# Result stores queued behind a step's gate weights, the last pair's products summed in PSUM, and a conversion's roundings in another order, in an fp32 attention and two-MoE kernel

## Chip, cores and metric

One core of one Trainium2 chip. The metric is the device time of one execution in microseconds. Before the change: a median of 1690.1 us over 3 runs, 1688.39 to 1690.28.

## What is computed

```python
scale = 1.0 / np.sqrt(64)
p_packed = sm_attn(p, k, v)              # p: (8, 8, 32, 64); k, v: (8, 8, 576, 64)
out = sm_attn(q, p_packed, p_packed)     # q: (8, 8, 576, 64)
x = out.transpose(0, 2, 1, 3).reshape(4608, 512)
...
h = x @ w_in                             # 512 x 2048
g = np.maximum(h, 0) + alpha * np.minimum(h, 0)
x = g @ w_out                            # 2048 x 512
...
g = x @ w_gate                           # 512 x 1536
silu = g * (1 / (1 + np.exp(-g)))
val = x @ w_val                          # 512 x 1536
return silu * val @ w_out                # 1536 x 512
```

`sm_attn` is a softmax attention with the scale above. Everything is float32.

## The kernel before

Every float32 product is made of three matmuls (`mm3`, lines 325 to 327): each operand is split into a rounded part `hi` and a remainder `lo`, and hi·hi, hi·lo and lo·hi are added in PSUM. ACT makes `hi` by a rounding copy, POOL makes `lo` by a subtraction.

**First part (up to about 790 us).** The attention, and the first MoE in 256 `h_unit`s and `o_unit`s. An `h_unit` multiplies on PE, ACT makes `m = alpha·h` (L1084), DVE makes `g = max(...)` (L1087), ACT rounds (L1095) and POOL subtracts (L1097); an `o_unit` multiplies `g` by `w_out` into four `acc` banks. The result goes to DRAM (`x1d`).

Between these units the weights of the second MoE are converted, in pieces that fill slots of the units (`all_weights2`, a generator whose `yield "s"`, `"p"` and `"a"` are pieces of one kind each). For each of 12 steps f, `piece2` takes a raw block through ACT, DVE and POOL (`widen`: ACT Abs L243, POOL L286) into a tile `g` or `v`; `less` (L1001, POOL) makes differences of blocks in place; `split2` (ACT L983, POOL L984, then a DMA) rounds one of the seven combinations and sends it to DRAM as `wgvd` (gate and value weights) or `wo2d` (output weights). For odd f, blocks of `w_out` follow.

**Second part (about 790 to 1659 us).** The second MoE runs in 6 blocks (NBLK) of 768 tokens with 12 steps (NF2) each, 72 calls of `gv_step`. A step makes a 2 x 2 block product by seven products instead of eight; `s1` and `s2` are its two results, silu · value for two token halves. Two steps are a pair m (36 pairs). Of each pair seven forms (OUT_FORMS: A11, S3, A12, S1, S2, A22, S4, sums and differences of its `s1`, `s2`) are multiplied by the output weights, in 14 units of 3 matmuls (e = 0, 1 for each form). Units of pair m stand in the steps 2m+1 and later, at places that UNITS and FIRST_UNIT set; `between(i)` in a step calls them. A step has 42 matmuls of its own products and 21 of units, 63 in all.

The first two forms are summed over a block's pairs in PSUM (`acc0` to `acc3`). The other five go to running totals, ten slots of two SBUF tiles `sums0`, `sums1` (`total`): DVE adds each product from PSUM (`more`, L1431). With a block's last pair the totals are combined with one another (A12, S2, A22, S4, S1), transposed by DVE (`put`, L1397) and sent out by SP, four stores of 48 KB for each of 8 transposes (L1401): 32 stores a block. For a block they fall in the first steps of the next one.

**Queues.** All these DMAs are issued by SP in program order, as the scheduler of the tile framework sets it. At the end of a step n `load_gv(n + 2)` (L1229) brings the gate weights of step n + 2 in two halves, into 4 buffers that hold two steps' weights. `load_wo2` (L1238) brings output weights of pair m + 2 behind units 7 and 13. `tc.issue_after(ins)` in the code keeps an instruction from being put ahead of `ins` by the scheduler.

Of the kernel before, what the change touches and what calls it, by code (L numbers as in the profile page):

```python
# [110 lines left out]
def tile_kernel(  # L111
# [37 lines left out]
    NQ = H // HQ  # L149
    NHALF = 2 * B  # L150
    NG = NF1 // WP

    ps = ctx.enter_context(tc.tile_pool(name="ps", bufs=1, space=PSUM))
    dram = ctx.enter_context(tc.tile_pool(name="dram", bufs=1, space=DRAM))
# [1061 lines left out]
    def table():  # L1216

        nc.scalar.activation(out=spare, in_=ident[:, :1], func=AF.Silu)

    def load_gv(n):  # L1220
        if n >= NBLK * NF2:
            return
        f = n % NF2
        gvw[n] = [
            wpool.tile([P, 7, 2 * P], F32R, tag="C", name=f"gv{n}_{t}", bufs=WBUFS["C"])
            for t in range(2)
        ]
        for t in range(2):
            nc.sync.dma_start(out=f32(gvw[n][t]), in_=wgvd[f][:, t])  # L1229

    def load_wo2(m, i):

        if m >= NBLK * NF2 // 2:
# [36 lines left out]
    def gv_step(n, between):  # L1270
# [45 lines left out]
        between(5)  # L1316
        next_x("S4")
        load_gv(n + 2)

        if s + 1 < NBLK:  # L1320
            with ExitStack() as held:
# [3 lines left out]
                    if f == d:  # L1325
                        prepare_x(s + 1, name)

    both, forms, outs = {}, {}, {}
# [31 lines left out]

    def forms_last(m):

        last = m == NBLK * NF2 // 2 - 1
        a12, a22 = both[2 * m + 1]
        s2 = both[2 * m][0]
        form(m, "A22", a22)
# [19 lines left out]
                    sums[n, k] = tiles[j][:, c * T : (c + 1) * T]  # L1386
        return sums[name, e]

    def put(s, name, e):

        t, dh = dict(A12=(0, 0), S4=(0, 1), A22=(1, 0), S1=(1, 1))[name]
        if not outs:
            outs["tile"] = vp.tile([P, 4, T], F32, tag="v", name="os")
            outs["n"] = 0
        o = outs["tile"][:, outs["n"] % 4]
        outs["n"] += 1
        nc.vector.transpose(out=o, in_=total(name, e))  # L1397
        r0 = (2 * s + t) * T
        for a in range(4):
            c = 256 * dh + P * e + 32 * a  # L1400
            nc.sync.dma_start(  # L1401
                out=out[r0 : r0 + T, c : c + 32].rearrange("(b j) i -> j b i", j=32),
                in_=o[32 * a : 32 * a + 32].rearrange("p (b i) -> p b i", i=32),
            )

    def out_unit(m, i):
# [5 lines left out]
        ends = m == NBLK * NF2 // 2 - 1  # L1412
        hi, lo = forms[m, name]
        w = wo2[m, k // 4][:, k % 4]
        c = slice(e * P, (e + 1) * P)
        keeps = k < 2
        bank = bank_of(f"acc{2 * k + e}" if keeps else ("h", "at")[e])
        with behind():
            ins = mm3(
                bank,  # L1420
                (w[:, 0, c], w[:, 1, c]),
                (hi, lo),
                first or not keeps,
                last or not keeps,
                skip_group_check=True,
            )
        done(ins)
        if e and k in (3, 6):
            load_wo2(m + 2, k // 4)
        def more(to, x, engine=nc.vector):  # L1430
            engine.tensor_tensor(out=total(to, e), in0=x, in1=total(to, e), op=ALU.add)  # L1431

        if keeps:
            for to in (("A12", "S2"), ("A22",))[k] if last else ():
                more(to, bank)
            return
        if first:
            nc.scalar.activation(out=total(name, e), in_=bank, func=AF.Copy)
        else:
            more(name, bank)  # L1440
# [12 lines left out]
        put(s, name, e)  # L1453

    due_at, after_at = {}, {}
    for m in range(NBLK * NF2 // 2):
        for i in range(2 * len(OUT_FORMS)):
            d = i + FIRST_UNIT
            if m == NBLK * NF2 // 2 - 1 and i == 3:
# [3 lines left out]
        after_at[2 * m + 2, 0] = lambda m=m: forms_later(m)  # L1463
        after_at[2 * m + 2, 1] = lambda m=m: forms_last(m)

    def out_next(n, i):

        for unit in due_at.pop((n, i), ()):
            out_unit(*unit)
        if (n, i) in after_at:  # L1470
            after_at.pop((n, i))()

# [34 lines left out]
    for n, i in sorted({*due_at, *after_at}):  # L1507
        out_next(n, i)


# [35 lines left out]
```

## Time and profile before

| | |
|---|---|
| median of 3 runs | 1690.1 us |
| profiled execution | 1688.99 us |
| its span, first to last instruction | 1686.8 us |
| mean granted clock of TensorE | 0.973 |
| DVE, POOL, ACT busy | 63%, 61%, 44% |
| DMA | 195 GB/s over the span |

The profiled execution is 2.2 us longer than its span. Of TensorE's clock 1.00 is full speed, 2.4 GHz, and 0.50 is 1.2 GHz. A row of a timeline gives the start, the duration, the engine, the line and the operation with its tiles (numbers left out); in brackets stands the engine's idle time before it and what ended that. Durations of neighbours overlap: matmuls of one row take .17 us from start to start. SPq is the queue of SP, whose durations are those of issuing.

### The profile page before, as it was taken

What the parts mean: (1) busy time and instruction counts of PE and PEld (TensorE: products, weight loads), DVE (VectorE), ACT (ScalarE), POOL (GpSimd) and SP (SyncE); (2) the same over time, 40 slices, a digit from 0 to 9 for tenths busy, and PEclk for the clock granted to TensorE, in tenths of its full rate; (3) what the DMA queues carried; (4) which work ended last, traced back from release to release, by engine and by line L of the source; (5) the groups of instructions that cost most, each with busy time, mean ns of one, the idle gap of its engine ahead of it and who ended that gap; (6) DMA issues with size and microseconds to landing.
All of it is one profiled execution on the core that took longest, in us unless ns stands there. A gap on an engine that the chain in (4) does not pass through costs nothing.

```text
span 1686.8 us, 30328 instructions
## 1 busy us (share of the span) xinstructions
PE 1575.8 (93%) x10925; PEld 1477.4 (88%) x10925; DVE 1070.5 (63%) x1886; ACT 741.0 (44%) x1666; POOL 1025.2 (61%) x1077
## 2 busy tenths in 40 slices
PE   6599999999999999999999989989999998998995
PEld 3467898889888898999999989989998998998994
DVE  6868667666757576673347836755684683675456
ACT  6575655555555555555333333333333333333321
POOL 4748666666666766765465656556674665566562
PEclk8699999999999999999999999999999999999998
DMA  9514365655555555454566866876677687667572
GB/s 281 140 46 138 94 187 138 171 136 153 142 150 145 149 160 131 146 184 133 214 237 247 272 222 251 299 238 237 248 249 269 252 283 246 245 237 255 219 262 38
DMA packets 304230, 330.73 MB, mean 196 GB/s; under 512 B 206016, under 2 KB 257232, under 8 KB 299472
## 3 DMA queue, kind: packets, MB, share of 16 engines
q1 hardware_dynamic: 304080, 328.80, 60.6%
q8 instruction: 86, 1.41, 0.3%
q14 instruction: 64, 0.52, 0.1%
HBM read 274.47 MB, written 54.26 MB: 195 GB/s over the span
## 4 chain that ended last, share of the span: by engine, by line
PE 66%; DVE 11%; DMA 8%; POOL 6%; issue 5%; ACT 3%; SPq 1%; DVEq 0%; POOLq 0%; ACTq 0%
PE acc L1110 5%; PE acc L1116 4%; PE acc L1111 4%; PE yb L325 4%; PE yb L326 4%; PE yb L327 4%; PE vb L326 3%; PE vb L325 3%; PE vb L327 3%; PE xb L325 3%; PE xb L326 3%; PE h L325 3%; PE xb L327 3%; DMA gv<-wgvd 2%; PE h L327 2%
## 5 line engine op out<-in xcount | busy, mean ns | idle before, releaser
L1097 POOL TENSOR_TENSOR lo<-g,hi 128x288 fp32r<-128x288 f32 x256 | 235.6, 921 | 228.5 <-ACT hi L1095 182.0
L1087 DVE SCALAR_TENSOR_TENSOR g<-h,sg,m 128x288 f32<-128x288 f32 x256 | 130.0, 510 | 175.7 <-ACT m L1084 152.0
L1312 POOL TENSOR_TENSOR s<-s,u 128x384 f32<-128x384 f32 x72 | 73.1, 1015 | 252.2 <-ACT s L1305 252.2
L1268 DVE TENSOR_TENSOR u<-yb,p 128x384 f32<-128x384 f32 x144 | 79.8, 554 | 199.1 <-PE yb L327 163.9
L325 PE MATMUL h<-a2h,ppw 128*128 128x288 f32 x512 | 161.4, 315 | 25.6 <-DVE g L1087 16.7
L1340 POOL TENSOR_TENSOR s<-s,s 128x384 f32<-128x384 f32 x141 | 149.2, 1058 | 46.3 <-DVE s L1309 40.8
L1095 ACT ACTIVATE hi<-g 128x288 fp32r<-128x288 f32 x256 | 113.2, 443 | 135.2 <-DVE g L1087 133.4
L325 PE MATMUL yb<-ring,gv 128*128 128x384 f32 x432 | 147.7, 342 | 9.1 <-DVE u L1268 9.1
L327 PE MATMUL h<-a2l,ppw 128*128 128x288 f32 x512 | 152.7, 299 | 2.2 <-POOL a2l L561 2.1
L326 PE MATMUL h<-a2h,ppw 128*128 128x288 f32 x512 | 152.7, 298 | 0.0
L1084 ACT ACTIVATE m<-h,sal 128x288 f32<-128x288 f32 x256 | 126.1, 495 | 56.7 <-PE h L327 55.8
L325 PEld LDWEIGHTS h<-a2h,ppw 128*128 128x128 f32 x512 | 97.9, 191 | 57.9 <-DVE g L1087 27.0
L1335 POOL TENSOR_TENSOR fl_S<-s,fh_S 128x384 fp32r<-128x384 f32 x144 | 146.4, 1027 | 0.1
L327 PE MATMUL yb<-ring,gv 128*128 128x384 f32 x432 | 146.1, 338 | 0.0
L326 PE MATMUL yb<-ring,gv 128*128 128x384 f32 x432 | 146.1, 338 | 0.0
L1268 DVE TENSOR_TENSOR u<-vb,u 128x384 f32<-128x384 f32 x144 | 79.8, 554 | 93.9 <-PE vb L327 93.9
L325 PE MATMUL xb<-ring,gv 128*128 128x384 f32 x288 | 101.4, 352 | 27.8 <-DMA gv<-wgvd 23.8
L1335 POOL TENSOR_TENSOR fl_A<-s,fh_A 128x384 fp32r<-128x384 f32 x108 | 111.7, 1034 | 25.0 <-ACT fh_A L1333 25.0
L1305 ACT ACTIVATE s<-p 128x384 f32<-128x384 f32 x72 | 37.8, 525 | 170.4 <-DVE p L1268 170.4
L1333 ACT ACTIVATE fh_S<-s 128x384 fp32r<-128x384 f32 x144 | 73.2, 519 | 78.8 <-POOL s L1340 76.4
L327 PEld LDWEIGHTS h<-a2l,ppw 128*128 128x128 f32 x512 | 97.8, 192 | 4.6 <-POOL a2l L561 3.7
L984 POOL TENSOR_TENSOR cva<-cva,cva 128x256 fp32r<-128x256 f32 x126 | 96.2, 773 | 6.2 <-ACT cva L983 6.2
(287 smaller groups left out, 4998.4 us busy)
## 6 DMA issues: line engine op xcount, KB each, us to landing
gv<-wgvd SPq DMA_DIRECT2D x144, 896.0 KB, 7.7
wp<-wo2d SPq DMA_DIRECT2D x36, 1024.0 KB, 5.2
wp<-wo2d SPq DMA_DIRECT2D x36, 768.0 KB, 4.4
wgvd<-cva SPq DMA_DIRECT2D x84, 256.0 KB, 2.7
wo2d<-cva SPq DMA_DIRECT2D x42, 256.0 KB, 2.5
v<-in_v_dram SPq DMA_DIRECT2D x16, 576.0 KB, 4.8
out_dram<-os SPq DMA_DIRECT2D x192, 48.0 KB, 1.8
cva<-in_moe_w_in_dram SPq DMA_DIRECT2D x7, 1024.0 KB, 7.6
```

Source lines behind the costliest of these rows:

```text
L325: nc.tensor.matmul(o, wlo, xhi, start=start, stop=False, **kw)
L326: nc.tensor.matmul(o, whi, xhi, start=False, stop=False, **kw)
L327: return nc.tensor.matmul(o, whi, xlo, start=False, stop=stop, **kw)
L984: nc.gpsimd.tensor_tensor(out=lo, in0=full, in1=f32(hi), op=ALU.subtract)
L1084: begun[it] = marks[f"u{it}"] = nc.scalar.activation(out=m, in_=hp, func=AF.Copy, scale=sal[:, f : f + 1])
L1087: made[it] = marks[f"m{it}"] = nc.vector.scalar_tensor_tensor(out=g32, in0=hp, scalar=sg[:, f : f + 1], in1=m, op0=ALU.mult, op1=ALU.max)
L1095: rounded[n] = nc.scalar.activation(out=hi, in_=x, func=AF.Copy)
L1097: nc.gpsimd.tensor_tensor(out=lo, in0=x, in1=f32(hi), op=ALU.subtract)
L1110: nc.tensor.matmul(acc[dc], lo[:, f % WP, c], ghi, start=start, stop=False)
L1268: return nc.vector.tensor_tensor(out=out, in0=bank, in1=x, op=ALU.add)
L1335: nc.gpsimd.tensor_tensor(out=lo, in0=x, in1=f32(hi), op=ALU.subtract)
L1340: engine.tensor_tensor(out=out, in0=x, in1=y, op=op)
```

## The change

- **Stores.** `put` only makes the transpose and notes the job. `store` issues the four stores of each job that is noted. It is called at a step's end, behind `load_gv(n + 2)`, and held behind that load's newest DMA. Transposes of A22 go to tiles of their own (`x`), those of A12, S4 and S1 to fixed slots of the one tile `os`; in the last block each has its own tile.
- **At a block's end** `S1 += S2` is made by DVE instead of POOL, ahead of `A22 += S2`.
- **The last pair.** Only the units of A11 and S3 are made as in other pairs. `out_last` adds all older totals first (10 adds on DVE), and then sums the products of the other forms in PSUM: a form that goes to two totals is multiplied twice (table LAST, 16 units, 48 matmuls instead of 30). Two `lo` of the last pair are made by DVE instead of POOL. Half of the last block's stores go to ACT's queue.
- **Conversion.** For odd f, two of the four `split`s come ahead of `piece2("g")` and two behind it, before all four ahead.

```diff
-            for k, full in (4, b11), (3, b12), (1, b22), (5, b21):
+            for k, full in (4, b11), (5, b21):
+                yield "s"
+                split(k, full)
+            if f % 2:
+                yield from piece2("g")
+            for k, full in (3, b12), (1, b22):
                 yield "s"
                 split(k, full)
@@
-            yield from piece2("g")
             yield "s"
             split_out("A11", b11)
@@ gv_step
         load_gv(n + 2)
+        store(n, 2)
@@ form
-        nc.gpsimd.tensor_tensor(out=lo, in0=x, in1=f32(hi), op=ALU.subtract)
+        by_dve = m == PAIRS - 1 and name in ("S2", "S4")
+        (nc.vector if by_dve else nc.gpsimd).tensor_tensor(out=lo, in0=x, in1=f32(hi), op=ALU.subtract)
@@ put
+        if s == NBLK - 1:
+            o = utile("u", [P, T], f"os{name}{e}_{s}")
+        elif name == "A22":
+            o = utile("x", [P, T], f"os{name}{e}_{s}")
+        else:
+            if not outs:
+                outs.append(vp.tile([P, 4, T], F32, tag="v", name="os"))
+            o = outs[0][:, 2 * (name == "S1") + e]
         nc.vector.transpose(out=o, in_=total(name, e))
+        stores.append((at_slot, o, (2 * s + t) * T, 256 * dh + P * e))
+        if s == NBLK - 1:
+            store(NBLK * NF2 + 9, 0)
+
+    def store(n, i):
+        for job in [j for j in stores if j[0] <= (n, i)]:
+            stores.remove(job)
+            at_slot, o, r0, c0 = job
+            with tc.issue_after(newest[-1].ins) if n < NBLK * NF2 else ExitStack():
+                for a in range(4):
+                    c = c0 + 32 * a
+                    queue = nc.scalar if a % 2 and n > NBLK * NF2 else nc.sync
+                    queue.dma_start(
...
@@ out_unit
         if name == "S1":
-            more("S4", total("S1", e))
-            more("S1", banks[f"acc{2 + e}"])
-            return
-        if name == "S2":
-            u2 = total("S2", e)
-            more("A22", u2)
-            more("S4", u2, nc.gpsimd)
-            more("S1", u2, nc.vector if ends else nc.gpsimd)
-            name = "S1"
-        put(s, name, e)
+            more("S4", e, total("S1", e))
+            more("S1", e, banks[f"acc{2 + e}"])
+        elif name == "S2":
+            u2 = total("S2", e)
+            more("S1", e, u2)
+            put(s, "S1", e, at_slot)
+            more("A22", e, u2)
+            more("S4", e, u2, nc.gpsimd)
+        else:
+            put(s, name, e, at_slot)
+
+    LAST = (
+        ("A12", "A12"), ("S1", "S1"), ("S1", "S4"), ("S2", "S1"), ("S2", "A22"), ("A22", "A22"),
+        ("S2", "S4"), ("S4", "S4"),
+    )
+
+    def out_last():
+        m = PAIRS - 1
+        forms_later(m)
+        forms_last(m)
+        for e in range(2):
+            more("S4", e, total("S1", e))
+            more("S1", e, banks[f"acc{2 + e}"])
+            for to in "S1", "A22", "S4":
+                more(to, e, total("S2", e))
...
+        for i, (name, to) in enumerate(LAST):
+            start = to not in [t for _, t in LAST[:i]]
+            stop = to not in [t for _, t in LAST[i + 1 :]]
+            for e in range(2):
+                unit(at_end[to, e], m, OUT_FORMS.index(name), e, start, stop)
+                if stop:
+                    more(to, e, at_end[to, e])
+                    put(NBLK - 1, to, e, (0, 0))
```

**SP at the first boundary between blocks** (steps 12 to 15). `gvN_0`, `gvN_1` are the gate weights of step N, `wpM` the output weights of pair M, `os` and `osA22` the transposes. Before:

```order
L1401 DMA out_0_dram<-os_12136 32x12x32 x8
L1238 DMA wp7_0_12185<-wo2d1_494 128x2048
L1229 DMA gv14_0_12233<-wgvd2_483 128x1792
L1229 DMA gv14_1_12234<-wgvd2_483 128x1792
L1401 DMA out_0_dram<-os_12136 32x12x32 x20
L1238 DMA wp7_1_12318<-wo2d1_494 128x1536
L1401 DMA out_0_dram<-os_12136 32x12x32 x4
L1229 DMA gv15_0_12354<-wgvd3_484 128x1792
L1229 DMA gv15_1_12355<-wgvd3_484 128x1792
L1238 DMA wp8_0_12440<-wo2d2_495 128x2048
L1229 DMA gv16_0_12470<-wgvd4_485 128x1792
L1229 DMA gv16_1_12471<-wgvd4_485 128x1792
```

After:

```order
L1245 DMA wp7_0_12177<-wo2d1_494 128x2048
L1236 DMA gv14_0_12217<-wgvd2_483 128x1792
L1236 DMA gv14_1_12218<-wgvd2_483 128x1792
L1423 DMA out_0_dram<-os_12136 32x12x32 x8
L1245 DMA wp7_1_12300<-wo2d1_494 128x1536
L1236 DMA gv15_0_12332<-wgvd3_484 128x1792
L1236 DMA gv15_1_12333<-wgvd3_484 128x1792
L1423 DMA out_0_dram<-os_12136 32x12x32 x8
L1423 DMA out_0_dram<-osA220_0_12254 32x12x32 x4
L1423 DMA out_0_dram<-osA221_0_12274 32x12x32 x4
L1423 DMA out_0_dram<-os_12136 32x12x32 x4
L1245 DMA wp8_0_12438<-wo2d2_495 128x2048
L1236 DMA gv16_0_12468<-wgvd4_485 128x1792
L1236 DMA gv16_1_12469<-wgvd4_485 128x1792
```

The 8 stores stood ahead of gv14 and stand behind it; the next 20 and 4 stood ahead of gv15, of which the 20 now stand behind it and ahead of gv16, and the 4 behind gv16.

**DVE at the same place.** `u2_13` is an operand of step 13's products, `sums0` and `sums1` hold the totals, L1309 (after: L1316) makes `s1` of step 12. Before:

```order
L1309 TENSOR_TENSOR s1_12_12092<-s1_12_12092,u2_12_12090 128x384
L1431 TENSOR_TENSOR sums1_10978<-sums0_10977,sums1_10978 128x384
L1431 TENSOR_TENSOR sums1_10978<-sums1_10978 128x384
L1268 TENSOR_TENSOR u2_13_12238<-yb13_12243,p1_13_12237 128x384
L1431 TENSOR_TENSOR sums1_10978<-o_h_10973,sums1_10978 128x384
L1397 STREAM_TRANSPOSE os_12136<-sums0_10977 128x384
```

After:

```order
L1316 TENSOR_TENSOR s1_12_12092<-s1_12_12092,u2_12_12090 128x384
L1429 TENSOR_TENSOR sums0_10977<-sums0_10977 128x384
L1429 TENSOR_TENSOR sums1_10978<-sums0_10977,sums1_10978 128x384
L1429 TENSOR_TENSOR sums0_10977<-sums1_10978,sums0_10977 128x384
L1429 TENSOR_TENSOR sums1_10978<-sums1_10978 128x384
L1275 TENSOR_TENSOR u2_13_12230<-yb13_12235,p1_13_12229 128x384
L1409 STREAM_TRANSPOSE os_12136<-sums0_10977 128x384
```

Two adds stood between `s1` and `u2_13`; now four do, and each has both operands in SBUF.

**POOL at the same place.** L1431 (after: L1429) are adds to the totals, `s3_6` and the `fl6` belong to the forms of pair 6. Before:

```order
L1431 TENSOR_TENSOR sums1_10978<-sums0_10977,sums1_10978 128x384
L1431 TENSOR_TENSOR sums0_10977<-sums0_10977 128x384
L1431 TENSOR_TENSOR sums1_10978<-sums1_10978 128x384
L1431 TENSOR_TENSOR sums0_10977<-sums1_10978,sums0_10977 128x384
L1340 TENSOR_TENSOR s3_6_12203<-s1_12_12092,s2_12_12093 128x384
L1335 TENSOR_TENSOR fl6_A11_12200<-s1_12_12092,fh6_A11_12198 128x384
L1335 TENSOR_TENSOR fl6_S3_12207<-s3_6_12203,fh6_S3_12205 128x384
```

After:

```order
L1429 TENSOR_TENSOR sums1_10978<-sums0_10977,sums1_10978 128x384
L1429 TENSOR_TENSOR sums1_10978<-sums1_10978 128x384
L1349 TENSOR_TENSOR s3_6_12195<-s1_12_12092,s2_12_12093 128x384
L1344 TENSOR_TENSOR fl6_A11_12192<-s1_12_12092,fh6_A11_12190 128x384
L1344 TENSOR_TENSOR fl6_S3_12199<-s3_6_12195,fh6_S3_12197 128x384
```

Two of the four adds have gone; what follows them is the same.

**POOL in the conversion**, at one odd step of the first MoE (L984, after L985: roundings; L1097, after L1102: the subtraction of an `h_unit`; L286, after L287: a piece of `widen`). Before:

```order
L1001 TENSOR_TENSOR cva0_104<-cva0_104 128x256
L984 TENSOR_TENSOR cva1_105<-cva0_104,cva1_105 128x256 x2
L1097 TENSOR_TENSOR lo95_4450<-g32_95_4444,hi95_4448 128x288
L984 TENSOR_TENSOR cva1_105<-cva0_104,cva1_105 128x256 x2
L1097 TENSOR_TENSOR lo96_4487<-g32_96_4481,hi96_4485 128x288
L1097 TENSOR_TENSOR lo97_4545<-g32_97_4539,hi97_4543 128x288
L1097 TENSOR_TENSOR lo98_4590<-g32_98_4584,hi98_4588 128x288
L286 TENSOR_TENSOR cva0_104<-cva0_104 128x512
```

After:

```order
L985 TENSOR_TENSOR cva1_105<-cva0_104,cva1_105 128x256
L1102 TENSOR_TENSOR lo95_4450<-g32_95_4444,hi95_4448 128x288
L985 TENSOR_TENSOR cva1_105<-cva0_104,cva1_105 128x256
L1102 TENSOR_TENSOR lo96_4487<-g32_96_4481,hi96_4485 128x288
L1102 TENSOR_TENSOR lo97_4542<-g32_97_4536,hi97_4540 128x288
L985 TENSOR_TENSOR cva1_105<-cva0_104,cva1_105 128x256
L287 TENSOR_TENSOR cva0_104<-cva0_104 128x512
L1102 TENSOR_TENSOR lo98_4584<-g32_98_4578,hi98_4582 128x288
L985 TENSOR_TENSOR cva1_105<-cva0_104,cva1_105 128x256 x2
```

Four roundings stood ahead of the piece's last addition, now three do: two of those of the step's gate weights moved, one of them behind it.

## Rows read from the trace of the kernel before

**Rows 1.** The page, busy time of each engine with its share of the span.
```profile
PE 1575.8 (93%) x10925; PEld 1477.4 (88%) x10925; DVE 1070.5 (63%) x1886; ACT 741.0 (44%) x1666; POOL 1025.2 (61%) x1077
```

**Rows 2.** Waits of PE, 700 to 1687 us: us in total, times, longest.
```profile
PE xb L325 <- DMA gv<-wgvd: 23.8, 5, 5.6
PE yb L325 <- DVE u L1268: 9.1, 10, 1.5
...
PE o_h L325 <- ACT fh_A L1333: 1.5, 1, 1.5
```

**Rows 3.** Timeline of PE at two boundaries: start, us, line, tiles, idle before.
```profile
962.41 0.45 PE L325 MATMUL yb<-ring,gv 128*128 128x384 f32 x1 [1.55 <-DVE u L1268]
...
969.87 0.34 PE L325 MATMUL xb<-ring,gv 128*128 128x384 f32 x1
...
980.66 0.34 PE L327 MATMUL o_at<-fl_S,wp 128*128 128x384 f32 x1
...
986.61 0.66 PE L325 MATMUL xb<-ring,gv 128*128 128x384 f32 x1 [5.61 <-DMA gv<-wgvd]
...
1272.63 0.66 PE L325 MATMUL xb<-ring,gv 128*128 128x384 f32 x1 [3.92 <-DMA gv<-wgvd]
```

**Rows 4.** Timeline of SP's queue at the first boundary.
```profile
952.32 3.93 SPq L1401 DMA_DIRECT2D out_dram<-os  x8
...
963.34 11.26 SPq L1401 DMA_DIRECT2D out_dram<-os  x20
...
975.20 1.98 SPq L1401 DMA_DIRECT2D out_dram<-os  x4
977.28 0.93 SPq L1229 DMA_DIRECT2D gv<-wgvd  x2
```

**Rows 5.** DMA issues of 956.5 to 958 and of 979.5 to 981: median us to landing.
```profile
gv<-wgvd SPq DMA_DIRECT2D x2, 896.0 KB, 7.8
...
gv<-wgvd SPq DMA_DIRECT2D x2, 896.0 KB, 12.0
```

**Rows 6.** Windows: length, busy times by engine, PEclk, DMA share, GB/s.
```profile
986.60:991.60 5.00, 4.99 (x16) 5.00 (x17) 0.56 (x1) 0.49 (x1) 0.00 (x0) 0.50 0.87 364
1272.60:1275.40 2.80, 2.77 (x9) 2.80 (x10) 0.00 (x0) 0.42 (x1) 0.00 (x0) 0.50 1.00 417
1557.50:1562.00 4.50, 4.48 (x14) 4.50 (x15) 0.21 (x1) 0.49 (x1) 0.00 (x0) 0.50 1.00 417
382.00:383.00 1.00, 1.00 (x6) 1.00 (x5) 1.00 (x3) 0.45 (x2) 0.30 (x1) 0.50 0.17 67
```

**Rows 7.** Timeline of DVE, at the first boundary and near the end.
```profile
959.25 1.37 DVE L1431 TENSOR_TENSOR sums<-sums,sums 128x384 f32<-128x384 f32 x1
...
961.82 0.55 DVE L1268 TENSOR_TENSOR u<-yb,p 128x384 f32<-128x384 f32 x1
...
1665.97 1.01 DVE L1431 TENSOR_TENSOR sums<-sums,sums 128x384 f32<-128x384 f32 x2
```

**Rows 8.** Timeline of POOL at the first boundary.
```profile
958.87 2.61 POOL L1431 TENSOR_TENSOR sums<-sums 128x384 f32<-128x384 f32 x2
```

**Rows 9.** Timeline of POOL, ACT and PE in the first MoE.
```profile
375.21 1.43 POOL L984 TENSOR_TENSOR cva<-cva,cva 128x256 fp32r<-128x256 f32 x2
...
376.68 0.67 ACT L243 ACTIVATE cva<-cva 128x512 f32<-128x512 f32 x1 [2.51 <-POOL cva L984]
...
379.97 0.40 PE L325 MATMUL h<-a2h,ppw 128*128 128x288 f32 x1 [2.49 <-DVE g L1087]
```

**Rows 10.** Timeline of DVE near the end.
```profile
1656.08 0.56 DVE L1431 TENSOR_TENSOR sums<-o_at,sums 128x384 f32<-128x384 f32 x1
...
1677.65 0.58 DVE L1397 STREAM_TRANSPOSE os<-sums 128x384 f32<-128x384 f32 x1 [1.50 <-DMA out_dram<-os]
```

**Rows 11.** Timeline of SP's queue at the end.
```profile
1664.70 19.69 SPq L1401 DMA_DIRECT2D out_dram<-os  x32
```

**Rows 12.** Waits of PE, 100 to 850 us.
```profile
PE h L325 <- DVE g L1087: 11.4, 11, 2.5
```

More of the change, by code (lines that the diff above doesn't have):

```diff
@@ L151, in tile_kernel @@
     NG = NF1 // WP
+    PAIRS = NBLK * NF2 // 2
     ps = ctx.enter_context(tc.tile_pool(name="ps", bufs=1, space=PSUM))
@@ L1218, in table @@
         nc.scalar.activation(out=spare, in_=ident[:, :1], func=AF.Silu)
+    newest = []
     def load_gv(n):
@@ L1228, in load_gv @@
         for t in range(2):
-            nc.sync.dma_start(out=f32(gvw[n][t]), in_=wgvd[f][:, t])
+            newest[:] = [nc.sync.dma_start(out=f32(gvw[n][t]), in_=wgvd[f][:, t])]
     def load_wo2(m, i):
-        if m >= NBLK * NF2 // 2:
+        if m >= PAIRS:
             return
@@ L1326, in gv_step @@
                         prepare_x(s + 1, name)
-    both, forms, outs = {}, {}, {}
+    both, forms, outs, stores = {}, {}, [], []
     def form(m, name, x):
@@ L1361, in forms_last @@
     def forms_last(m):
-        last = m == NBLK * NF2 // 2 - 1
+        last = m == PAIRS - 1
         a12, a22 = both[2 * m + 1]
@@ L1387, in total, with put @@
         return sums[name, e]
-    def put(s, name, e):
+    def put(s, name, e, at_slot):
         t, dh = dict(A12=(0, 0), S4=(0, 1), A22=(1, 0), S1=(1, 1))[name]
[L1392 to L1396, printed above, removed]
-        nc.vector.transpose(out=o, in_=total(name, e))
[L1398 to L1403, printed above, removed]
-            )
@@ new lines, in store @@
+    def store(n, i):
[7 more added lines that the diff above has]
+                    queue.dma_start(
+                        out=out[r0 : r0 + T, c : c + 32].rearrange("(b j) i -> j b i", j=32),
+                        in_=o[32 * a : 32 * a + 32].rearrange("p (b i) -> p b i", i=32),
+                    )
@@ new lines, in more, with unit, out_unit @@
+    def more(to, e, x, engine=nc.vector):
+        engine.tensor_tensor(out=total(to, e), in0=x, in1=total(to, e), op=ALU.add)
+    def unit(bank, m, k, e, start, stop):
+        hi, lo = forms[m, OUT_FORMS[k]]
+        w = wo2[m, k // 4][:, k % 4]
+        c = slice(e * P, (e + 1) * P)
+        with behind():
+            last = mm3(
+                bank, (w[:, 0, c], w[:, 1, c]), (hi, lo), start, stop, skip_group_check=True
+            )
+        done(last)
+    def out_unit(m, i, at_slot):
@@ L1411, in out_unit @@
         first, last = r == 0, r == NF2 // 2 - 1
[L1412 to L1415, printed above, removed]
         keeps = k < 2
         bank = bank_of(f"acc{2 * k + e}" if keeps else ("h", "at")[e])
[L1418 to L1427, printed above, removed]
+        unit(bank, m, k, e, first or not keeps, last or not keeps)
         if e and k in (3, 6):
             load_wo2(m + 2, k // 4)
-        def more(to, x, engine=nc.vector):
-            engine.tensor_tensor(out=total(to, e), in0=x, in1=total(to, e), op=ALU.add)
         if keeps:
             for to in (("A12", "S2"), ("A22",))[k] if last else ():
-                more(to, bank)
+                more(to, e, bank)
             return
@@ L1439, in out_unit @@
         else:
-            more(name, bank)
+            more(name, e, bank)
         if not last:
@@ L1443, in out_unit @@
         if name == "S1":
-            more("S4", total("S1", e))
-            more("S1", banks[f"acc{2 + e}"])
-            return
-        if name == "S2":
+            more("S4", e, total("S1", e))
+            more("S1", e, banks[f"acc{2 + e}"])
+        elif name == "S2":
             u2 = total("S2", e)
-            more("A22", u2)
-            more("S4", u2, nc.gpsimd)
-            more("S1", u2, nc.vector if ends else nc.gpsimd)
-            name = "S1"
-        put(s, name, e)
+            more("S1", e, u2)
[7 more added lines that the diff above has]
+        ("S2", "S4"), ("S4", "S4"),
+    )
+    def out_last():
[7 more added lines that the diff above has]
+                more(to, e, total("S2", e))
+        at_end = {}
+        for tag, to in ("", "A12"), ("free", "S1"), ("acc0", "S4"), ("acc2", "A22"):
+            for e in range(2):
+                if tag == "free":
+                    name = ("h", "at")[e]
+                    at_end[to, e] = ps.tile([P, 512], F32, tag=name, name=f"oe{e}", bufs=2)[:, :T]
+                else:
+                    at_end[to, e] = banks[f"acc{int(tag[3:]) + e}" if tag else ("h", "at")[e]]
+        for i, (name, to) in enumerate(LAST):
+            start = to not in [t for _, t in LAST[:i]]
+            stop = to not in [t for _, t in LAST[i + 1 :]]
+            for e in range(2):
+                unit(at_end[to, e], m, OUT_FORMS.index(name), e, start, stop)
+                if stop:
+                    more(to, e, at_end[to, e])
+                    put(NBLK - 1, to, e, (0, 0))
     due_at, after_at = {}, {}
-    for m in range(NBLK * NF2 // 2):
-        for i in range(2 * len(OUT_FORMS)):
+    for m in range(PAIRS):
+        for i in range(4 if m == PAIRS - 1 else 2 * len(OUT_FORMS)):
             d = i + FIRST_UNIT
-            if m == NBLK * NF2 // 2 - 1 and i == 3:
+            if m == PAIRS - 1 and i == 3:
                 d -= 1
@@ L1462, in tile_kernel @@
             due_at.setdefault((2 * m + 1 + n, UNITS[u]), []).append((m, i))
-        after_at[2 * m + 2, 0] = lambda m=m: forms_later(m)
-        after_at[2 * m + 2, 1] = lambda m=m: forms_last(m)
+        if m < PAIRS - 1:
+            after_at[2 * m + 2, 0] = lambda m=m: forms_later(m)
+            after_at[2 * m + 2, 1] = lambda m=m: forms_last(m)
     def out_next(n, i):
-        for unit in due_at.pop((n, i), ()):
-            out_unit(*unit)
+        for job in due_at.pop((n, i), ()):
+            out_unit(*job, (n, i))
         if (n, i) in after_at:
@@ L1506, in tile_kernel @@
         gv_step(n, lambda i, n=n: out_next(n, i))
-    for n, i in sorted({*due_at, *after_at}):
-        out_next(n, i)
+    assert not due_at and not after_at
+    out_last()
 _INS = [
```

1 line of the change is left out of this document (removed).

## Prediction

> **What bounds the kernel now.** I read the page's busy times first, then the waits of PE, then the timelines round the places where PE waits. PE is busy 93% of the span [rows 1], and no other engine comes near, so a change can only gain where PE waits or runs slowly. The stretch of the second MoE (700 to 1687 us) is the one that the diff touches most. There PE waits 23.8 us for gate weights, in 5 waits, and 9.1 us for DVE's `u`, in 10 [rows 2]. Five waits are the five boundaries between blocks. At the first one, step 14 starts at 969.87 and its last matmul at 980.66, and the next step's first matmul stands at 986.61, after 5.61 us of waiting [rows 3]. A step of 63 matmuls thus takes 10.8 us plus the last one's .17, that is 11.0.
>
> Why the weights of step 15 are late is in the queue of SP [rows 4]. SP issues 8 stores in 3.93 us (.49 each), 20 stores in 11.26 us (.56 each), one load of `wp`, 4 more stores, and only then, at 977.28, the two halves of gv15, 3.4 us before step 15 could begin. The weights take 7.8 us from issue to landing right behind a load of `wp`, and 12.0 when two steps' weights are under way together [rows 5].
>
> The wait costs twice. Behind each of the five the granted clock is 0.50 (the 1.2 GHz level) for a while: 5.0 us, 5.0, 2.8, 3.5 and 4.5, together 20.8 us, of which the first, the third and the last stand in [rows 6]. Half of that is lost: 10.4 us. PE had been busy without a gap until each wait.
>
> **What the change removes at the boundaries.** The order of SP puts gv14 ahead of the first 8 stores and gv15 ahead of the 20. gv15 then waits only for the buffers of gv13, which step 13's last gate product frees at about 968.8. I put its issue at 969.2 and its landing at 977.0, against a need at 980.66. So the wait goes: −23.8 us, and the clock behind it: −10.4.
>
> **What is late next.** gv16 now stands behind 20 stores and `wp8_0`. In the built program each DMA of SP waits until the eighth one before it has landed, so the seventh store waits for gv15, to 977.0; 14 stores of .5 us (between the .49 and .56 above) end at 984.0, `wp8_0` adds about another .5, and gv16 goes out at about 984.5. Landing takes 7.8 (the row behind a `wp` load, which is its place now) to 12.0. It lands at 992.3 to 996.5, against a need at 980.7 + 11.0 = 991.7. I take the near row, which has the same neighbours: .6 late, five times, **+3**. The far end is 4.8 late, five times, +24.
>
> **What the change adds on DVE.** At the boundary DVE now has four adds of two SBUF operands ahead of `u2` of step 13 instead of two, and POOL two fewer. In the trace of before the two adds run from 959.25 to `u2` at 961.82, so each holds DVE for 1.285 us [rows 7], while POOL runs its own adds in 1.31 each [rows 8]. The same adds without POOL's take 1.01 for two, .46 from start to start [rows 7]. DVE and POOL thus take turns. POOL still has work for the whole time, since its two remaining adds, `s3_6`, `fl6_A11` and `fl6_S3` follow at once. Two more adds make `u2` 2 × 1.285 = 2.57 us later. PE already waits 1.55 us for that `u2` [rows 3], so there is no slack: the wait becomes 4.1, five times 2.57: **+12.9**. Nothing is late on POOL for it.
>
> The Trainium skill (SBUF — State Buffer, "SBUF: two separate sides") says the port pair that VectorE, for an operation with two SBUF inputs, and GpSimd share is an exclusive lock, held for a whole instruction, so that the other blocks fully. That speaks against this part, and the doubled spacing in [rows 7] agrees. The rule does not say who comes next when both wait. If DVE kept its turn, the four adds would take 1.9 us, and the part would gain rather than cost; the rows show turns, and I go by them.
>
> A wait of 4.1 us would also lower the clock. The nearest wait in the trace, 3.92 at 1272.63 [rows 3], was followed by 2.8 us at 0.50 [rows 6], so 1.4 lost, five times: **+7**. The ends are the last boundary with its 4.5 us (2.25 lost each, +11), and 2.49 in the first MoE, with about 1 us (.5 lost, +2.5) [rows 6, 9].
>
> **The end of the kernel.** Before, DVE's last transpose stands at 1677.65 [rows 10] and SP issues 32 stores from 1664.70 for 19.69 us [rows 11], to 1684.39; the span ends 2.4 us later. So SP sets the end. After, DVE has 39 operations from the same add at 1656.08 on, 38 before. At .47 they end at 1674.4; I add 2.6 for adds with POOL in between, as two of them cost above. The last transpose at 1677.0 has only two stores on each of two queues behind it, 1.0 us, then the 2.4: 1680.4, a gain of 6.4. The price of a store on ACT's queue is in no row; I take SP's. If it were double, the end would be 1 us later. The sum in PSUM means 48 matmuls on PE in place of 30. They are covered by DVE at .174 each (8.4 us), but PE will stand idle ahead of them: its 1.5 us of waiting for `fh_A` [rows 2] grows by the four added DVE operations ahead of that form (4 × .47), to 3.4. If the clock falls behind that, they take 16.8 us at the 0.50 level and set the end at 1683.7, a gain of 3.1. Between the two I take **−5**. Below zero it hardly goes, as SP's 32 stores alone held the end.
>
> **The conversion in the first MoE.** PE waits there for `g` 11 times, 11.4 us [rows 12]. The longest, 2.49, begins because ACT's Abs of a weight piece at 376.68 waits 2.51 for POOL's two roundings at 375.21 (1.43 for two), and the `m` behind it waits too [rows 9]. I put about half of the 11.4, 5.8, down to such pieces of odd steps. The change moves two of the four roundings behind the piece, so that the piece waits for two less. If they all go, that is 5.8 and about 1 of clock. The moved roundings come due later beside other work, and could bring back as much. I take **−4**, with ends −7 and +3.
>
> The bookkeeping in Python, the other tiles for the transposes and the moved `load_gv` statement issue no instruction of their own: 0. The A22 transposes go to buffers of x tiles; were one not free yet, a transpose and what DVE has behind it would wait, and I have no row for that.
>
> **The sum** against the profiled execution (1688.99): −23.8 − 10.4 + 3 + 12.9 + 7 − 5 − 4 = −20.3, so **1668.7 us**. The median of the runs is 1.1 above that execution.
>
> **Rivals.**
> *The four adds cost PE nothing* (POOL finds nothing to run beside them, or DVE keeps its turn). For it: uncontended adds at .46 in [rows 7], and four of these are shorter than two of now. Against it: POOL's three successors. Then +12.9 and +7 fall away: 1648.8. Half of it, a longer wait with no clock behind it, gives 1661.7.
> *Slower: the gate weights are late one step further on.* gv16 behind 20 stores lands 4.8 us after its need, as with the 12.0 us of [rows 5], instead of .6. That is +21 over my sum, and a loss of clock like the fourth boundary's (half of 3.5 us) comes with it, +8.8: 1668.7 + 30 = 1699. It decides from a landing of some 11 us on: 3.8 late is +16 and +7, 1692, where the gain is gone. For it: the wait is only moved down the queue, past work of the same size. Against it: nothing but stores and one `wp` load is under way with gv16 now, while the row with 12.0 had gv15 too.
> *The change doesn't free gv15:* if the stores were still ahead of it in the queue, only tail and conversion would move: −9 and +20 from DVE, 1700. The built order shows gv15 ahead, so this has next to no chance.
> *Only part of it:* gv16 late by 2 us (+7) and the moved roundings giving their gain back (+7): 1683, still faster.
>
> **How the numbers follow.** Forecast with its own bounds (1660 to 1680): .57. Adds that cost nothing, 1649: .22. Partial, around 1683: .09. A sum of losses that comes back to the time of before: .05. Late gv16 or a worse loss, 1692 and up: .07. The range from 1646 (the first rival with the tail's and the conversion's better ends) to 1685 takes in the first three, .88 less their edges. What a measurement can tell from no change is about 0.2%, 3.4 us: faster .88, within it .05, slower .07.
>
> **What would show it.** In the profile after: no wait of `xb` for gv15, with gv15 issued at about 969 and gv16 at 984.5; if PE waits for gv16, step 16's first row shows how long. The `u2` at a boundary about 5.2 us behind the first of the four adds, with PE waiting 4 us before `yb` and the clock at 0.50 behind it, five times; 2 us and no long wait would mean that the first rival holds. The last transpose near 1677 less what was gained before it, and half as many stores on SP after it. The two roundings behind the piece, with fewer of PE's waits for `g`. The prediction is wrong if the time is below 1660 (DVE's adds were priced wrongly) or above 1680 (the queue or the clock was).

## The result, and the profile after the change

The change is slower: a median of 1709.1 us over 4 runs (1704.1 to 1712.0), against 1690.2 for the kernel before, a ratio of 1.011 with a 95% interval of 1.0085 to 1.0136. The profiled execution took 1710.2 us, 21.2 more than that of before.

PE is busy the same share of a longer span. The page's busy times:

```profile
PE 1590.0 (93%) x10943; PEld 1493.3 (87%) x10943; DVE 1098.1 (64%) x1898; ACT 739.6 (43%) x1666; POOL 1012.0 (59%) x1063
```

Where the 21 us are is read from two matmuls in the timeline of PE, the first of step 0 and the first of step 71 of the second MoE. Before:

```profile
817.84 0.34 PE L325 MATMUL xb<-ring,gv 128*128 128x384 f32 x1
...
1647.53 0.34 PE L325 MATMUL xb<-ring,gv 128*128 128x384 f32 x1
```

After:

```profile
822.67 0.34 PE L326 MATMUL xb<-ring,gv 128*128 128x384 f32 x1
...
1672.93 0.34 PE L326 MATMUL xb<-ring,gv 128*128 128x384 f32 x1
```

The first part of the program lost 4.8 us, the steps with their five boundaries another 20.6 (25.4 less 4.8), and the end won back 3.8 of its span (25.4 less the 21.6 by which the span grew, from 1686.8 to 1708.4). Lengths of steps away from the boundaries are unchanged, 11.0 to 11.8 us.

Waits of PE after, 700 to 1710 us, which answer to [rows 2] (us in total, times, longest):

```profile
PE xb L326 <- DMA gv<-wgvd: 21.9, 5, 5.2
PE yb L326 <- DVE u L1275: 21.7, 10, 4.1
...
PE o_h L326 <- ACT fh_A L1341: 3.3, 1, 3.3
```

The wait for `u` grew as forecast, from 1.55 to 4.1 at each boundary. The wait for gate weights, which was to vanish, is still there, in five waits and nearly at its old sum. It belongs to another step. PE's timeline at the first boundary, with the wait for `u` in step 13 and that for gate weights ahead of step 16 (before: ahead of step 15 [rows 3]):

```profile
969.79 0.44 PE L326 MATMUL yb<-ring,gv 128*128 128x384 f32 x1 [4.08 <-DVE u L1275]
...
1004.46 0.66 PE L326 MATMUL xb<-ring,gv 128*128 128x384 f32 x1 [3.59 <-DMA gv<-wgvd]
```

SP's queue at the same place, which answers to [rows 4]:

```profile
977.57 0.82 SPq L1236 DMA_DIRECT2D gv<-wgvd  x2
978.48 9.15 SPq L1423 DMA_DIRECT2D out_dram<-os  x8
987.73 4.00 SPq L1423 DMA_DIRECT2D out_dram<-osA  x8
991.82 1.95 SPq L1423 DMA_DIRECT2D out_dram<-os  x4
993.87 0.41 SPq L1245 DMA_DIRECT2D wp<-wo2d  x1
994.38 1.81 SPq L1236 DMA_DIRECT2D gv<-wgvd  x2
```

gv15 goes out at 977.57, with the last gate product of step 13, and PE doesn't wait for it. The 20 stores behind it (9.15, 4.00 and 1.95 us with the gaps) hold SP until 993.87, and gv16 goes out at 994.38, 10.1 us ahead of the matmul that waited for it. Single rows of the first eight of these stores show where SP was held: the fourth to the sixth took 1.9 to 2.7 us each, the other five .38 to .47. The seventh went out at 986.65; gv15's second half, issued at 978.01, took 8.8 us and so landed at about 986.8. The fourth, fifth and sixth:

```profile
979.94 1.85 SPq L1423 DMA_DIRECT2D out_dram<-os  x1
...
981.89 2.00 SPq L1423 DMA_DIRECT2D out_dram<-os  x1
...
983.94 2.66 SPq L1423 DMA_DIRECT2D out_dram<-os  x1
```

The clock fell behind both waits of each boundary. Windows, with the columns of [rows 6]: behind the first boundary's wait for gate weights, and behind the second boundary's for `u`.

```profile
1004.60:1007.60 3.00, 3.00 (x10) 3.00 (x11) 0.00 (x0) 0.78 (x2) 0.00 (x0) 0.50 1.01 412
1115.00:1119.00 4.00, 4.00 (x12) 4.00 (x13) 2.93 (x6) 0.00 (x0) 0.00 (x0) 0.50 0.17 29
```

DVE's timeline at the first boundary, which answers to [rows 7]. Four adds run from 964.10 to `u` at 969.19, 1.27 each:

```profile
964.10 1.37 DVE L1429 TENSOR_TENSOR sums<-sums 128x384 f32<-128x384 f32 x1
965.39 2.62 DVE L1429 TENSOR_TENSOR sums<-sums,sums 128x384 f32<-128x384 f32 x2
967.93 1.34 DVE L1429 TENSOR_TENSOR sums<-sums 128x384 f32<-128x384 f32 x1
969.19 0.55 DVE L1275 TENSOR_TENSOR u<-yb,p 128x384 f32<-128x384 f32 x1
```

POOL's operations at the same time start between them, every 1.27 us too:

```profile
965.01 1.31 POOL L1349 TENSOR_TENSOR s<-s,s 128x384 f32<-128x384 f32 x1
966.28 1.30 POOL L1344 TENSOR_TENSOR fl_A<-s,fh_A 128x384 fp32r<-128x384 f32 x1
```

In the first MoE, the waits of PE for `g`, 100 to 850 us, are 17.2 us in 14, before 11.4 in 11 [rows 12]:

```profile
PE h L326 <- DVE g L1092: 17.2, 14, 2.3
```

### The profile page after: what moved, and what is told of

Read it like the earlier page. It is cut to its first block, busy times and chain, and to the rows that moved or that the text cites. A ratio compares the mean times of both kernels' runs of the same rounds, so it can differ in the third digit from the quotient of the medians.

```text
span 1708.4 us, 30336 instructions
## 1 busy us (share of the span) xinstructions
PE 1590.0 (93%) x10943; PEld 1493.3 (87%) x10943; DVE 1098.1 (64%) x1898; ACT 739.6 (43%) x1666; POOL 1012.0 (59%) x1063
## 4 chain that ended last, share of the span: by engine, by line
PE 70%; DVE 11%; DMA 6%; issue 4%; POOL 4%; ACT 2%; SPq 1%; DVEq 0%; POOLq 0%; ACTq 0%
PE acc L1115 6%; PE acc L1121 5%; PE acc L1116 5%; PE yb L326 4%; PE yb L328 4%; PE yb L327 4%; PE h L326 3%; DMA gv<-wgvd 3%; PE xb L326 3%; PE h L328 3%; PE h L327 3%; DVE sums L1429 3%; PE vb L326 3%; PE vb L327 3%; PE vb L328 3%
## 5 line engine op out<-in xcount | busy, mean ns | idle before, releaser
L1102 POOL TENSOR_TENSOR lo<-g,hi 128x288 fp32r<-128x288 f32 x256 | 233.1, 912 | 227.4 <-ACT hi L1100 187.3
L326 PE MATMUL yb<-ring,gv 128*128 128x384 f32 x432 | 149.9, 347 | 21.7 <-DVE u L1275 21.7
L1344 POOL TENSOR_TENSOR fl_S<-s,fh_S 128x384 fp32r<-128x384 f32 x142 | 145.4, 1032 | 25.4 <-ACT fh_S L1341 25.1
L327 PE MATMUL yb<-ring,gv 128*128 128x384 f32 x432 | 147.8, 342 | 0.0
L328 PE MATMUL yb<-ring,gv 128*128 128x384 f32 x432 | 147.7, 342 | 0.0
L326 PE MATMUL xb<-ring,gv 128*128 128x384 f32 x288 | 101.1, 351 | 25.9 <-DMA gv<-wgvd 21.9
L326 PEld LDWEIGHTS yb<-ring,gv 128*128 128x128 f32 x432 | 83.7, 194 | 26.1 <-DVE u L1275 26.1
L985 POOL TENSOR_TENSOR cva<-cva,cva 128x256 fp32r<-128x256 f32 x126 | 96.9, 778 | 10.2 <-ACT cva L984 9.6
```

The lines of the kernel that those rows point to most:

```text
L326: nc.tensor.matmul(o, wlo, xhi, start=start, stop=False, **kw)
L327: nc.tensor.matmul(o, whi, xhi, start=False, stop=False, **kw)
L328: return nc.tensor.matmul(o, whi, xlo, start=False, stop=stop, **kw)
L985: nc.gpsimd.tensor_tensor(out=lo, in0=full, in1=f32(hi), op=ALU.subtract)
L1344: (nc.vector if by_dve else nc.gpsimd).tensor_tensor(out=lo, in0=x, in1=f32(hi), op=ALU.subtract)
```

## Experiments

The theory after the result: SP's queue carries the wait on. What is put behind one step's weights stands ahead of the next one's, and the queue part as a whole gives nothing; the adds on DVE cost what was forecast; the conversion costs some 3 to 5 us and the end gives some 4 to 6. The rivals: gate weights land late because of the stores' packets beside them, wherever these stand in the queue; and what looks like cost of the conversion is scatter.

### One part at a time

**The queue alone.** `put` and `store` as in the change; the adds, the end and the conversion as before. Against the change (the two main places; the lines that undo the conversion and the rest of the end are left out):

```diff
-            more("S1", e, u2)
-            put(s, "S1", e, at_slot)
             more("A22", e, u2)
             more("S4", e, u2, nc.gpsimd)
+            more("S1", e, u2, nc.vector if m == PAIRS - 1 else nc.gpsimd)
+            put(s, "S1", e, at_slot)
...
-    assert not due_at and not after_at
-    out_last()
+    for n, i in sorted({*due_at, *after_at}):
+        out_next(n, i)
```

> The kernel before with the stores queued as in the change and nothing else of it (no add moved to DVE, the old end, the old conversion). Theory: the wait moves from the gate weights of step 15 to those of step 16 and keeps its size, so the time stays within 3 us of the kernel before, about 1690 us. Rival (what was forecast of this part): the wait and the clock behind it go, but for 3 us: about 1659.

Measured: 1686.7 us, ratio 0.9994 (0.9981 to 1.0008), no difference. The theory holds: the five waits for gate weights are 19.8 us, against 23.8 before. The waits, and SP's queue at the first boundary, show the change's picture without its other parts: gv16 goes out 16.7 us behind gv15, and PE waits.

```profile
PE xb L326 <- DMA gv<-wgvd: 19.8, 5, 4.4
```

```profile
967.09 0.83 SPq L1232 DMA_DIRECT2D gv<-wgvd  x2
...
983.77 1.73 SPq L1232 DMA_DIRECT2D gv<-wgvd  x2
```

**The adds.** The change with S1 += S2 back on POOL.

```diff
-            more("S1", e, u2)
-            put(s, "S1", e, at_slot)
             more("A22", e, u2)
             more("S4", e, u2, nc.gpsimd)
+            more("S1", e, u2, nc.gpsimd)
+            put(s, "S1", e, at_slot)
```

> The change with S1 += S2 at a block's end back on POOL. Theory: PE's five waits for u fall from 4.1 to 1.5 us (12.6 us) and the clock at 0.50 behind them goes (about 10 us), while the waits for gate weights of some 4 us stay where they are: about 1687. Rival: PE then only comes earlier to gate weights that land when they did, so that the waits for them grow by the same 2.5 us: about 1700 or more.

Measured: 1687.0 us, ratio to before 0.9982 (0.9973 to 0.9992), 22 us below the change. Waits of PE, 700 to 1690:

```profile
PE xb L326 <- DMA gv<-wgvd: 22.1, 5, 5.9
PE yb L326 <- DVE u L1275: 9.0, 10, 1.5
```

The waits for `u` are what they were before, and those for gate weights haven't moved. The rival (they grow by the same amount) falls.

**The end.** The kernel before with `out_last` and its stores alone. Against the change (with S1 += S2 and the conversion as before, too):

```diff
         load_gv(n + 2)
-        store(n, 2)
...
-        if s == NBLK - 1:
-            store(NBLK * NF2 + 9, 0)
+        store(NBLK * NF2 + (9 if s == NBLK - 1 else 0), 0)
```

> The kernel before with the new end of the program alone (last pair summed in PSUM, half of its stores on ACT's queue); stores, the adds at the boundaries and the conversion are as before. Theory: 4.2 us less, as the two traces differ behind the last step, so about 1686. Rival: the end's gain came from the state in which the last step was reached, and alone it gives 0 to 1 us.

Measured: 1684.1 us, ratio 0.9964 (0.9948 to 0.9979), 6.1 us less, between 3.5 and 8.8.

**The conversion.** The kernel before with the new order alone.

```diff
-            for k, full in (4, b11), (3, b12), (1, b22), (5, b21):
+            for k, full in (4, b11), (5, b21):
+                yield "s"
+                split(k, full)
+            if f % 2:
+                yield from piece2("g")
+            for k, full in (3, b12), (1, b22):
                 yield "s"
                 split(k, full)
```

> The kernel before with the conversion's new order alone. Theory: the first part of the program, which ended 4.8 us later in the profile of the change, is late because of this order, so about 1690 + 5 = 1695 us, with PE's waits for g some 6 us more than the 11.4 of before. Rival: the 4.8 us are the scatter of executions, and the order as such gives what was forecast, 1686, or nothing, 1690.

Measured: 1692.9 us over 10 runs, ratio 1.0017 (1.0008 to 1.0027), 2.9 us more, so it isn't scatter. The waits for `g` are 16.3 us, against 11.4. The timelines of ACT, DVE and PE at the odd step of [rows 9]:

```profile
373.88 0.42 ACT L983 ACTIVATE cva<-cva 128x256 fp32r<-128x256 f32 x1 [2.35 <-POOL cva L1001]
...
376.04 0.68 ACT L243 ACTIVATE cva<-cva 128x512 f32<-128x512 f32 x1 [0.26 <-POOL cva L984]
```

```profile
379.18 0.68 DVE L258 SCALAR_TENSOR_TENSOR cva<-cva 128x512 uint32<-128x512 uint32 x1
379.90 1.01 DVE L267 TENSOR_SCALAR cva<-cva 128x512 uint32<-128x512 uint32 x1
380.94 1.09 DVE L276 SCALAR_TENSOR_TENSOR cva<-cva 128x512 f32<-128x512 uint32 x1
381.96 0.51 DVE L1091 SCALAR_TENSOR_TENSOR g<-h,sg,m 128x288 f32<-128x288 f32 x1
```

```profile
382.52 0.61 PE L325 MATMUL h<-a2h,ppw 128*128 128x288 f32 x1 [2.14 <-DVE g L1091]
```

The Abs of the piece waits .26 us instead of 2.51, as forecast. But the rounding ahead of it (L983) now comes to ACT before POOL's last difference is made and waits 2.35 for it, and the piece's operations on DVE now run three in a row (L258, L267, L276), where `g` stood between them before; PE waits 2.14 for the `g` behind them.

**Three roundings ahead of the piece.** The kernel before with the order 4, 3, 5, piece, 1. It was meant to take the 2.35 away and keep part of the gain.

```diff
-            for k, full in (4, b11), (3, b12), (1, b22), (5, b21):
+            for k, full in (4, b11), (3, b12), (5, b21):
                 yield "s"
                 split(k, full)
+            if f % 2:
+                yield from piece2("g")
+            yield "s"
+            split(1, b22)
```

> The kernel before with three of the four roundings (4, 3, 5) ahead of the piece and one (1) behind it. Theory: in the change's order ACT comes to the rounding of the block that POOL's last difference makes too early and waits for it, with the activation of an h unit behind it; with one rounding between them that wait goes, and the piece waits for one rounding less than before: 1687 to 1690 us. Rival: any rounding behind the piece costs more there than it saves ahead: 1692 or more.

Measured: 1699.7 us, ratio 1.0066 (1.0047 to 1.0084): 11 us more than before, and worse than two and two. The forecast gain isn't there, but the run doesn't test ACT's wait alone: at the same odd step ACT still waits 1.81 ahead of that rounding, and the Abs waits 2.09 again.

```profile
373.67 0.42 ACT L983 ACTIVATE cva<-cva 128x256 fp32r<-128x256 f32 x1 [1.81 <-POOL cva L1001]
...
376.51 0.67 ACT L243 ACTIVATE cva<-cva 128x512 f32<-128x512 f32 x1 [2.09 <-POOL cva L984]
```

Where the 11 us are can be read: PE's waits for `g` are 17.6 us, 6.2 more than before, and behind the waits of 2.14 at three more odd steps (565, 657 and 749 us) the clock is at 0.50 for at least 2.6 to 2.9 us, half of which is lost, some 4 us together. At these steps it stayed at 1.00 before. The waits, and one such window here and at the same step before:

```profile
PE h L325 <- DVE g L1090: 17.6, 12, 2.1
```

```profile
565.10:568.00 2.90, 2.90 (x12) 2.90 (x13) 1.58 (x5) 2.02 (x5) 2.82 (x4) 0.50 0.90 295
```

```profile
563.20:566.00 2.80, 2.80 (x19) 2.60 (x20) 2.80 (x6) 2.35 (x6) 1.61 (x2) 1.00 0.00 0
```

The same edit on the best version (below):

> The best version so far (adds on POOL, held behind u, stores in two places) with that order of the conversion: 0 to 3 us below 1642.6 by the theory, 2 or more above it by the rival.

Measured: 1656.1 us, ratio 0.9809 (0.9788 to 0.983), 13.5 us above that version. What roundings behind the piece cost is shown by these runs. The way in which they do it is read from the rows only: DVE's three operations in a row, with the wait of 2.14 behind them, stand in both orders, but no run takes them apart.

### Is it the place in the queue, or the packets?

**Four stores a step.** The change with at most one job of `store` at a step's end. In the output of this kernel one of a block's eight transposed tiles, the second of A12, is replaced by S4's that shares its slot.

```diff
-        for job in [j for j in stores if j[0] <= (n, i)]:
+        for job in [j for j in stores if j[0] <= (n, i)][: 1 if n < NBLK * NF2 else None]:
```

> The change with at most four stores behind the gate weights of a step's end, so that the 32 of a block spread over eight steps. Theory: the gate weights are late because SP's stores wait in the queue, the seventh behind a load for that load to land; four never do, so no wait for gate weights is left (21.9 us and some 11 of clock less): about 1677, with the waits for u at 4.1 as they are. Rival: the weights are late because they land slowly beside the stores' small packets; four stores then still stand beside every load, landing stays near 10 us, and half of the waits remain: about 1693.

Measured: 1674.7 us, ratio 0.9905 (0.9887 to 0.9922). No wait for gate weights is left.

**Eight a step, in two places.** The same, with a second call of `store` early in each step, ahead of the transposes of S4.

```diff
         if (n, i) in after_at:
             after_at.pop((n, i))()
+        if i == 1 and n < NBLK * NF2 and newest:
+            store(n, 1)
```

> The change with its stores put in two places of a step, four behind the gate weights of the step's end and four in the step's middle, so that a block's 32 are out before the next loads need the queue. Theory (the loads were late because they stood behind up to 20 stores): no wait for gate weights, as with four a step, about 1675 us. Rival (landing is slowed by the stores' packets beside it, twice as many here as with four a step): waits for gate weights come back, 1680 or more.

Measured: 1674.7 us, ratio 0.9913 (0.9897 to 0.9929). PE's waits, 700 to 1670, begin with those for `u`, 21.7 us as in the change; none for gate weights is among them. Below them is SP's queue at the first boundary, with the issue of gv16's second half:

```profile
979.08 0.82 SPq L1236 DMA_DIRECT2D gv<-wgvd  x2
979.99 5.71 SPq L1423 DMA_DIRECT2D out_dram<-os  x4
985.80 3.66 SPq L1423 DMA_DIRECT2D out_dram<-osA  x4
...
990.07 0.85 SPq L1236 DMA_DIRECT2D gv<-wgvd  x2
```

```profile
gv<-wgvd SPq DMA_DIRECT2D x1, 896.0 KB, 10.8
```

Eight stores still take 9.4 us behind gv15, as in the change. But then it is gv16's turn, 11.0 us behind gv15 instead of 16.8, one step's length. The stores are the same and stand beside the loads as before. gv16's second half, issued at 990.54, even lands more slowly here (10.8 us, in the change 8.5), and PE still doesn't wait for it. So landing can be slower with stores beside it, but it's the place in the queue that decides.

### A version that beats both

**Two places, adds on POOL, old conversion.** The last kernel with two edits from above undone in it.

```diff
+            more("S1", e, u2, nc.gpsimd)
...
+            for k, full in (4, b11), (3, b12), (1, b22), (5, b21):
```

> The same with S1 += S2 back on POOL and the conversion in its old order. Theory: against the kernel before, the gate weights' waits (23.8) and the clock behind them (10.4) go and the end is 5.5 shorter, so about 1690 - 34 - 5.5 = 1650; against the run above, 12.6 us of waits for u with some 6 of clock and 3 of the conversion. Rival: PE meets another wait at the boundaries that those covered (the next u, the x tiles or gate weights of the step after): 1660 or more.

Measured: 1649.1 us, ratio 0.9758 (0.9741 to 0.9775). Against the run with the end alone (0.9964) that is some 35 us less. For the waits for gate weights and the clock behind them the prediction had 34.2: its price was right, once no other load is late in gv15's place.

**The adds held behind the next step's `u`.** The same; what S2 of a block's last pair adds to the other totals is issued at the first place of the next step, behind its `u`.

```diff
+    def s2_adds(s, e, u2):
+        at_slot = (0, 0)
+        more("A22", e, u2)
+        more("S4", e, u2, nc.gpsimd)
+        more("S1", e, u2, nc.gpsimd)
+        put(s, "S1", e, at_slot)
@@ out_next
+        if i == 0:
+            while later:
+                with tc.issue_after(u2_made[-1].ins):
+                    later.pop(0)()
```

> The run above with the adds that a block's last S2 brings held behind the next step's u. Theory: PE's five waits of 1.55 us for u fall to the .3 of other steps, 6 us less: about 1644. Rival: the adds come in the way of the next u or the chain of s and forms instead, and nothing is gained: 1650.

Measured: 1642.6 us, ratio 0.9725 (0.971 to 0.9739), the fastest kernel here, 47 us below the one before. Waits of PE ahead of `yb`, 700 to 1670: five of .3 us for `u`; none for weights.

```profile
PE yb L326 <- DVE u L1271: 1.4, 5, 0.3
```

**The same with S1 += S2 on DVE.**

```diff
-        more("S1", e, u2, nc.gpsimd)
+        more("S1", e, u2)
```

> The same with S1 += S2 on DVE as in the change. Theory: what the four adds on DVE cost in the change was their place ahead of u, and behind it they are hidden: within 2 us of the run above. Rival: DVE taking turns with POOL for 5 us costs PE a wait wherever they stand: 10 us or more above it.

Measured: 1659.2 us, ratio 0.9832 (0.9806 to 0.9857), 17 us above the run before it; here the rival holds. DVE's and PE's timelines at the first boundary:

```profile
956.28 0.68 DVE L1425 TENSOR_TENSOR sums<-sums 128x384 f32<-128x384 f32 x1
956.88 2.65 DVE L1425 TENSOR_TENSOR sums<-sums,sums 128x384 f32<-128x384 f32 x2
...
961.22 0.51 DVE L1425 TENSOR_TENSOR sums<-o_h,sums 128x384 f32<-128x384 f32 x1
```

```profile
961.78 0.45 PE L326 MATMUL o_h<-fh_S,wp 128*128 128x384 f32 x1 [3.02 <-DVE sums L1425]
```

The four adds take turns with POOL here too, from 956.28 to 960.72, 4.4 us instead of 5.1. Behind `u` they hold up DVE's next read of the bank `o_h`, at 961.22, and PE waits 3.0 us for that bank, at each of the five boundaries.

## Why the prediction was wrong

The measured time lies outside the range, and the sign was wrong: the rival with .07, gate weights late one step further on, is what happened. By its own steps:

- **gv15 (−23.8 and −10.4): right.** It went out with step 13's last gate product, and PE never waits for it.
- **What is late next (+3): this step failed, by the landing time that was put into it.** It had gv16 .6 us late; PE waited 3.59 us at the first boundary and 21.9 in all, with a clock of 0.50 behind each wait, instead of 3 and none. Its 7.8 us from issue to landing is a median over the two halves of a load, each counted from its own issue, but PE needs both halves. In the trace of before gv15 went out at 977.28 and its matmul came at 986.61 [rows 3, 4], 9.3 us later. The second half was issued at 977.82 and took 8.7, so it landed at about 986.5, .1 ahead of that matmul:

```profile
gv<-wgvd SPq DMA_DIRECT2D x1, 896.0 KB, 8.7
```

  The 7.8 stands in the sum twice, ahead of the seventh store and behind gv16's issue; with 9.3 the same sum gives 3.6 us late. The trace of the change bears the places out, part by part: the seventh store went out 9.1 us behind gv15 instead of 7.8 (it didn't wait itself; the three ahead of it were slow to issue), the other 14 and the `wp` load took 7.7 instead of 7.5, and gv16's matmul came 10.1 behind its issue instead of 7.8. The need came .8 later than forecast, 23.3 us behind gv15's issue. That 3.6 comes out to the tenth is luck, as this .8 and the .8 by which 10.1 is above 9.3 cancel. The queue part was forecast at −31 and gives −1 by the run with it alone (−3.2 to +1.4). The prediction saw the other end, 4.8 us late, and took the near one. The rival had +30 for this part, which is what came; its 1699 was still short of the measured time, for the most part by the conversion (+2.9 instead of −4).
- **The adds on DVE (+12.9 and +7): right in its mechanism and place.** `u` is 2.5 us later each time (1.27 per add against 1.285). The clock's part was undersized: 2.8 us at 0.50 were taken for each, and the windows behind the five waits are 3.7, 5.3, 5.5, 3.4 and 6.1 us at 0.50 to 0.55. About 11.8 us are lost in them, where 7 were forecast. Together +20 were forecast; taking the add back gave 22.
- **The rule of the exclusive port pair** (the Trainium skill, SBUF — State Buffer, "SBUF: two separate sides") agrees with the 1.27 us per add while POOL has work, against .46 without. That the engines take turns, which the rule leaves open, was shown again by the run with the adds behind `u`.
- **The end (−5): right in size,** −6.1 alone, 3.8 of the span in the trace of the change. DVE's last transposes and the end of ACT's queue in the trace of the change:

```profile
1701.15 1.01 DVE L1409 STREAM_TRANSPOSE osS<-sums 128x384 f32<-128x384 f32 x2
```

```profile
1703.23 2.10 ACTq L1423 DMA_DIRECT2D out_dram<-osS  x4
```

  The second of the two transposes starts at 1701.63, which is 1676.2 in the time of before (25.4 less); forecast was 1677.0. A store on ACT's queue takes .53, so SP's price was right for it. PE's wait for `fh_A` came out as forecast, 3.3 against 3.4. But the span ends at 1683.0 in the time of before, 2.6 later than forecast: the last transpose has four stores on ACT's queue behind its start, not two, since those of the transpose ahead of it hadn't gone out yet.
- **The conversion (−4): wrong in sign,** +2.9. The wait that it named went from 2.51 to .26, and two others came (above). The forecast had named this bound, +3.

The parts add up: −1 for the queue, +2.9 for the conversion and −6.1 for the end, each alone against the kernel before, and +22 for the adds, taken out of the change, are +18; the change measured +19.

## What to carry to other kernels

Work that is moved behind a load in an in-order queue stands ahead of the next load: reckon the queue through a whole period, and ask whether it is empty when the next load may start. Count a load that is issued in parts from its first issue to its last landing; a median over the parts is too short. Here the same 32 stores were harmless once no more than eight stood between two loads, and 20 in one place cost as much as before. Two engines that take turns on one resource made an add cost 1.3 us on either of them, so moving one over gained nothing. What gained some 6 us was to hold the adds, still on POOL, behind what the bounding engine waits for.

## What was not expected

Stores behind a gate-weight load are slow to issue: some .47 us each elsewhere, but 1.9 to 2.7 us for the fourth to the sixth behind gv15 in the change, until about when the load has landed. In the run with two places the fourth alone takes 4.24. SP itself is held, in the trace of the change and in that of every version that puts stores there. What holds it, these runs do not show.

The clock at 0.50 lasted longer behind some waits for `u` of 4.06 to 4.08 us than behind others. Behind the first boundary's wait, at 969.79, it is back at 1.00 by 973.60; behind the second's, at 1115.00, it is still at 0.50 from 1119.00 on, with the same matmuls. Why, these runs do not show.

```profile
973.60:975.00 1.40, 1.40 (x10) 1.40 (x9) 1.18 (x3) 0.00 (x0) 0.00 (x0) 1.00 0.00 0
1119.00:1120.30 1.30, 1.30 (x6) 1.30 (x6) 0.98 (x2) 0.00 (x0) 0.00 (x0) 0.50 0.00 0
```
